# Starting product 2 of a tile inside the same tile: a new hand-written order of TensorE and ScalarE in a convolution and two-matmul kernel

## The chip, the cores and the metric

The kernel runs on one core of a Trainium2 chip. The metric is the time on the device, in microseconds (us), of one execution; smaller is better. A profile of one execution gives, for each engine, when every instruction started and ended. The engines are named as the profile names them: PE is TensorE (PEld its weight loads), ACT is ScalarE, DVE is VectorE, POOL is GpSimd, and SP is the engine whose queue issues the transfers (DMA).

## What is computed

The input `x` has 8 sequences of 4096 tokens with 192 features. Step one is a causal convolution over the last 7 tokens, with softmax-normalised weights of 8 heads (24 features each). Step two is a gated feed-forward layer on the 32768 tokens, with 2048 hidden features:

```python
w = exp(weight - max); w = w / (sum(w) + 1e-09)      # per head, 7 taps
x = einsum('hk,bskhg->bshg', w, x_unf)               # causal, zero-padded
h = x @ w_in                                         # 192 -> 2048
g = h * np.cos(h)
out = g @ w_out                                      # 2048 -> 192
```

## The kernel before

**Tiles and units.** The tokens are cut into 64 tiles of 512 (`T`, `NT`). Loads, the convolution and the transposition work on units of 1024 tokens, two tiles each (`U`, `TPU`), so there are 32 units.

**The way of one unit.** SP loads `x` (`load_unit`, `load_edges`). POOL casts it to bf16 (`cast_unit`, L174). PE convolves it as matmuls against a banded weight matrix (`conv_mm`, L185), in two parts of four heads; each part takes two PSUM banks and is cut in two steps, `c1` and `c2` (for a second part in the same tile `d1` and `d2`), between which the two row halves of PE change banks. ACT copies both banks out (`conv_out`, L200; written `ec` or `ed` in the order of ACT). POOL doubles the result (`double_unit`, L236), the DMA transposes it into `cT` (`turn_unit`, L242), and POOL mends the first six tokens of each 128 (`mend_edges`, L248).

**The way of one tile.** Product 1 makes eight slots `h0` to `h7` (`mm1`, L322), each of six matmuls of 512 columns and two PSUM banks. For each slot ACT computes the cosine (`s0` to `s7`, L328) and DVE multiplies it with h into the tile `g` (called g0 to g7 below, L332). Product 2 (`mm2_step`, L352) consists of 64 steps a tile, each of two matmuls of 192 columns that run side by side on the two row halves of PE. It runs in phases of 32 steps; in a phase the upper row half works on one half tile of the output and the lower row half on the half tile of the phase before. The results collect in two single-bank pools, `o_p` and `o_q`. ACT copies them out (`evac`, L364), `P` for half 0 and `Q` for half 1, and SP stores them.

**What sets the order.** Every engine works its own queue in order, and the order of the loop is written by hand: `PE_ORDER` and `ACT_ORDER` for tiles from 2 on, `PE_FIRST` and `ACT_FIRST` for tiles 0 and 1. In `PE_ORDER`, `m8` means eight steps of product 2.

```python
    PE_ORDER = "h0 c1 m8 c2 h1 m8 h2 h3 m16 | h4 h5 m8 h6 m12 h7 m12"
    ACT_ORDER = "P s0 ec s1 s2 s3 Q s4 s5 s6 s7"
```

In tile t the kernel before computes product 1 of tile t and product 2 of tile t-1 (upper rows) with the rest of tile t-2 (lower rows). Two more rounds follow the last tile.

**Buffers.** `h_pool` is a ring of three pairs of PSUM banks, taken in turn by the slots of product 1 and by the convolution. So a slot waits until the third one before it is free: `h2` waits for g0 of its own tile, because h0, the convolution and h1 hold the three pairs in between; `c1` waits for g6 of the tile before, and `h1` for g7. `cos_pool` and `gpool` have three buffers, the pools of `x`, its cast, `ct` and `cT` two each.

**Turns.** [...] Where they change banks, class `Turn` puts a small marker on SP's queue (L158): it waits for the last matmul of one half, and the first matmul of the other waits for it. The marker stands in SP's queue behind whatever transfers were issued before it.

Of the kernel before, what the change touches and what calls it, by code (L numbers as in the profile page):

```python
# [8 lines left out]
FP32 = mybir.dt.float32  # L9
# [7 lines left out]
def kernel(  # L17
# [8 lines left out]
    nc = tc.nc  # L26
# [5 lines left out]
    T = 512  # L32
    NT = NTOK // T
    NB = T // 128
    U = 1024
    NU = NTOK // U
    UB = U // 128
    UPS = S // U
    TPU = U // T
    NF = Dff // 128  # L40
    NP = NF // 2
# [25 lines left out]
    def load_edges(u):  # L67
        nc.sync.dma_start(out=x_tiles[u][:, UB, :],
                          in_=xf[u * U - 8 : u * U - 8 + U, :].rearrange("(n t) d -> n t d", t=128)[:, 0:16, :])
# [12 lines left out]
    HP = NP // 2  # L82
# [8 lines left out]
    def load_wo(q):  # L91
        for i in range(2):
            nc.sync.dma_start(out=wo_f[:, q * HP : (q + 1) * HP, i], in_=wo_src[:, q * HP : (q + 1) * HP, i])

    load_edges(1)
    load_wo(0)


    one = consts.tile([128, 128], FP32)
# [69 lines left out]
    def cast_unit(u, n0=0, n1=UB + 1):  # L169
        copy = nc.scalar.copy if u == 0 and n0 == 0 else nc.gpsimd.tensor_copy  # L170
        bf[u] = xb0 if u == 0 else xbf_pool.tile([128, UB + 1, D], BF16, name="x_bf")

        o = 1 if u == 0 else 0
        copy(out=bf[u][:, n0 + o : n1 + o, :].rearrange("p n (h k r) -> p (n h) k r", k=NC, r=R),  # L174
             in_=x_tiles[u][:, n0:n1, :].rearrange("p n (h r k) -> p (n h) k r", k=NC, r=R))
        if u and u % UPS == 0:
            nc.gpsimd.memset(bf[u][0:8, UB, :], 0.0)
        bf.pop(u - 2, None)
# [9 lines left out]
            rhs=bf[u][rows, n0:n1, h * G : (h + 1) * G].rearrange("p n (k r) -> p n k r", k=NC),  # L188
            skip_group_check=True, **flags)

    def conv_out(u, c, ps, n0, m0, m1, copy, double=False):

        for b in range(2):
            w0 = (2 * c + b) * 2 * R
            o = ct_tiles[u][:, m0:m1, :, :, w0 : w0 + 2 * R].rearrange("p n k t w -> p (n k) t w")
            i = ps[b][:, (m0 - n0) * 2 * G : (m1 - n0) * 2 * G].rearrange("p (m t w) -> p m t w", t=1, w=2 * R)
            if double:
                copy(o, i.to_broadcast([128, (m1 - m0) * NC, 2, 2 * R]))  # L198
            else:
                copy(o[:, :, 0, :], i[:, :, 0, :])  # L200

    def ring_banks():
        h = h_pool.tile([128, 2, T], FP32, name="h")
        return [h[:, 0, :], h[:, 1, :]]
# [4 lines left out]
    def conv_part(u, c, banks):  # L209


        ps = banks()
        sides = [slice(0, 64), slice(64, 128)]

        def mm(i, rows, **flags):
            return conv_mm(u, c, ps, i, sides[rows], 0, UB + 1, **{"start": False, "stop": False, **flags})

        mm(0, 0, start=True)
        mm(2, 1, start=True)
        turn = Turn()  # L220
        turn.mark(mm(1, 0), mm(3, 1))
        yield
        turn.wait(mm(2, 0), mm(0, 1))
        mm(3, 0, stop=True)
        mm(1, 1, stop=True)
        yield
        if c == 0 and u not in ct_tiles:
            ct_tiles[u] = ct_pool.tile([128, UB + 1, NC, 2, 64], BF16, name="ct")
        conv_out(u, c, ps, 0, 0, UB + 1, nc.scalar.copy)
        yield  # L230

    cT = {}

    def double_unit(u, n0=0, n1=UB + 1):
        ct = ct_tiles[u]
        nc.gpsimd.tensor_copy(out=ct[:, n0:n1, :, 1, :], in_=ct[:, n0:n1, :, 0, :])  # L236

    def turn_unit(u, n0=0, n1=UB + 1):
        ct = ct_tiles.pop(u)
        if u not in cT:  # L240
            cT[u] = cT_pool.tile([128, UB + 1, NC, 128], BF16, name="cT")
        nc.sync.dma_start_transpose(out=cT[u][:, n0:n1].rearrange("p n c k -> p (n c) k"),  # L242
                                    in_=ct[:, n0:n1].rearrange("p n c t k -> p (n c t k)"))
        cT.pop(u - 2, None)
# [52 lines left out]
    list(b)  # L297
    for half in range(2):
        list(across[half])
    double_unit(0, NB, UB)  # L300
    turn_unit(0, NB, UB)
    load_wo(1)
    nc.gpsimd.tensor_copy(out=w[:, :, HP:NP], in_=w_f[:, :, HP:NP])
    cast_unit(1)
    for q in range(2):
        nc.gpsimd.tensor_copy(out=wo[:, q * HP : (q + 1) * HP], in_=wo_f[:, q * HP : (q + 1) * HP])  # L306
    load_unit(2)
    load_edges(2)


    g_tiles = {}
# [23 lines left out]

    STEPS = 2 * NF

    def mm2_step(t, q):
        half, i = divmod(q, STEPS)
        f, si = divmod(i, 2)  # L340
        for r, (tt, b) in enumerate(((t - 1, half), (t - 1, 0) if half else (t - 2, 1))):
            if not 0 <= tt < NT:
                continue
            if r == 0 and i == 0:
                if tt < NT - 1:
                    o_ps[tt, b] = o_pools[b].tile([128, T], FP32, name="o_ps%d" % b)
                elif b == 0:

                    o_ps[tt, 0], o_ps[tt, 1] = ring_banks()
            rows = slice(64 * r, 64 * r + 64)  # L350
            s = 2 * b + si
            m = nc.tensor.matmul(out=o_ps[tt, b][:, si * D : (si + 1) * D],  # L352
                                 lhsT=g_tiles[tt][rows, f, s * 128 : (s + 1) * 128], rhs=wo[rows, f // 2, f % 2, :],
                                 start=(r == 0 and i == 0), stop=(r == 1 and i == STEPS - 1), skip_group_check=True)
            if r == 0 and i == STEPS - 1:
                turns[tt, b] = Turn()
                turns[tt, b].mark(m)
            if r == 1 and i == 0:
                turns.pop((tt, b)).wait(m)

    def evac(t, b):
        if b == 0:
            o_sb[t] = opool.tile([128, NB, D], FP32, name="o_sb")
        nc.scalar.copy(o_sb[t][:, 2 * b : 2 * b + 2, :].rearrange("p s d -> p (s d)"), o_ps.pop((t, b))[:, 0 : 2 * D])  # L364
# [6 lines left out]

    PE_ORDER = "h0 c1 m8 c2 h1 m8 h2 h3 m16 | h4 h5 m8 h6 m12 h7 m12"
    ACT_ORDER = "P s0 ec s1 s2 s3 Q s4 s5 s6 s7"

    PE_FIRST = ["h0 h1 h2 h3 h4 d1 h5 d2 h6 c1 h7 c2 |", "h0 m8 h1 m8 h2 h3 m16 | h4 c1 h5 m8 c2 h6 m12 h7 m12"]
    ACT_FIRST = ["s0 s1 s2 s3 s4 s5 ed s6 s7 ec", "s0 s1 s2 s3 s4 s5 ec s6 s7"]

    for t in range(NT + 2):  # L380
        u, second = divmod(t, TPU)
        cu, cc = (u + 2, 0) if second else (u + 1, 1)
        conv = {"c": conv_part(cu, cc, ring_banks if t else o_banks) if cu < NU else iter(())}
        if t == 0:
            conv["d"] = conv_part(1, 0, o_banks)
        act, done, h, step = (ACT_ORDER if t > 1 else ACT_FIRST[t]).split(), set(), {}, 0

        def flush():
            while act:
                k = act[0]  # L390
                need = {"P": "start", "Q": "|", "e": k[1:] + "2"}.get(k[0], "h" + k[1:])
                if need not in done:
                    return
                act.pop(0)
                if k == "P" and 0 <= t - 2 < NT:
                    evac(t - 2, 0)
                    if t == NT + 1:
                        store(t - 2, 0, 1)
                elif k == "Q" and 0 <= t - 2 < NT:
                    evac(t - 2, 1)  # L400
                elif k[0] == "e":
                    next(conv[k[1]], None)
                elif k[0] == "s" and t < NT:
                    gcu(t, int(k[1:]), h.pop(int(k[1:])))

        done.add("start")
        flush()
        for k in (PE_ORDER if t > 1 else PE_FIRST[t]).split():
            if k[0] == "h" and t < NT:
                h[int(k[1:])] = mm1(t, int(k[1:]))  # L410
            elif k[0] in conv:
                next(conv[k[0]], None)
            elif k[0] == "m":
                for q in range(step, step + int(k[1:])):
                    mm2_step(t, q)
                step += int(k[1:])
            done.add(k)
            flush()

            if k == ("|" if t == 0 else "h1") and second == 0 and cu < NU:  # L420
                double_unit(cu)
            if k == "|":
                if second == 0 and cu < NU:
                    turn_unit(cu)
                if 0 <= t - 2 < NT:
                    store(t - 2, 1 if t == NT + 1 else 0)
                if second == 1 and u + 3 < NU:
                    load_unit(u + 3)
                    load_edges(u + 3)
                if second == 0 and u + 2 < NU:  # L430
                    cast_unit(u + 2)
                if second == 0 and cu < NU:
                    mend_edges(cu)


# [28 lines left out]
```

## Time and profile before

The median of three runs is 734.67 us (734.67 to 735.29). The profiled execution spans 733.8 us.

| stage of the profile | us | PE busy | DVE busy | ACT busy |
|---|---|---|---|---|
| start to h0 of tile 2 (0 to 37.53) | 37.53 | 30.73 | 28.37 | 25.87 |
| tiles 2 to 62 (37.53 to 710.03) | 672.50 | 670.50 | 580.50 | 593.47 |
| tile 63 and the rest (710.03 to the end) | 23.77 | 19.24 | 10.92 | 11.06 |

Each line is one stretch of time with the microseconds that each engine was busy in it. Matmuls are pipelined and their ends are modelled by the profiler, so a busy PE can still hold waits. The starts of matmuls are therefore the better clock: two equal points of neighbouring tiles lie 11.04 us apart in the long middle stage.

### The profile page before, as it was taken

To read this page: it belongs to the slowest core of one execution; us is meant where nothing else is said; L and a number is where in the kernel's file an instruction comes from. 1 tells how busy PE (TensorE), PEld (TensorE's weight loads), DVE (VectorE), ACT (ScalarE), POOL (GpSimd) and SP (SyncE) were. 2 spreads that over 40 slices of the span, in tenths; PEclk is the share of its full clock that TensorE was granted. 3 is DMA by queue.
4 is the path that set the end of the run, shared out by engine and by line. 5 is a ranking of instruction groups with operands and counts; after the bars stand their busy time and mean duration, and the time that the engine had idled before them with its cause. 6 is when DMAs were issued, how large, how long until landed. Compare 5 with 4: busy or idle time off the path is not lost.

```text
span 733.8 us, 26364 instructions
## 1 busy us (share of the span) xinstructions
PE 720.5 (98%) x11835; PEld 546.5 (74%) x11835; DVE 619.8 (84%) x537; ACT 630.4 (86%) x781; POOL 150.0 (20%) x119
## 2 busy tenths in 40 slices
PE   7899999999999999999999999999999999999997
PEld 3577777777777777777777777777777777777776
DVE  6888888888888888888888888888888888888883
ACT  5888888888988988988988988988988988988883
POOL 4422220222210222211222211222211222211100
PEclk9999999999999999999999999999999999999999
DMA  9725435535335345446345345355345345343401
GB/s 226 202 74 142 112 101 142 108 105 142 108 106 142 101 113 141 88 127 142 97 116 142 97 117 141 93 121 127 107 123 142 89 125 141 88 126 94 93 24 67
DMA packets 184075, 86.04 MB, mean 117 GB/s; under 512 B 111642, under 2 KB 183194, under 8 KB 183962
## 3 DMA queue, kind: packets, MB, share of 16 engines
q1 hardware_dynamic: 183960, 84.36, 44.1%
q8 instruction: 92, 1.51, 0.8%
q14 instruction: 21, 0.17, 0.1%
q10 hardware_dynamic: 2, 0.00, 0.0%
HBM read 31.36 MB, written 25.17 MB: 77 GB/s over the span
## 4 chain that ended last, share of the span: by engine, by line
PE 97%; DVE 1%; ACT 1%; issue 1%
PE h L322 46%; PE o_ps L352 46%; PE h L185 3%; PE o_ps L107 1%; DVE g L332 1%; PE h L352 1%; ACT cs L328 0%; ACT ct L200 0%; ACT ct L198 0%; DVE cT L289 0%; ACT o_sb L364 0%; PE h L285 0%; PE o_ps L114 0%; PE o_ps L185 0%; DVE zero L102 0%
## 5 line engine op out<-in xcount | busy, mean ns | idle before, releaser
L332 DVE TENSOR_TENSOR g<-h,cs 128x1024 bf16<-128x1024 f32 x512 | 609.1, 1221 | 97.5 <-ACT cs L328 86.2
L328 ACT ACTIVATE cs<-h 128x1024 bf16<-128x1024 f32 x512 | 511.5, 1025 | 80.8 <-PE h L322 79.4
L352 PEld LDWEIGHTS <-g 64*128 64x128 bf16 x8192 | 362.4, 94 | 68.0 <-ACT ct L200 1.2
L322 PE MATMUL h<-cT,w 64*128 64x512 bf16 x3072 | 401.2, 376 | 5.5 <-DVE g L332 2.1
L352 PE MATMUL o_ps<-wo,g 64*128 64x192 bf16 x8064 | 403.2, 243 | 0.7 <-ACT ct L200 0.7
L322 PEld LDWEIGHTS <-w 64*128 64x128 bf16 x3072 | 166.5, 94 | 92.8 <-issue 15.4
L236 POOL COPY ct<-ct 128x1728 bf16<-128x1728 bf16 (+1 forms) x32 | 51.4, 1605 | 377.3 <-ACT ct L200 374.2
L174 POOL CAST x_bf<-x_f 128x1728 bf16<-128x1728 f32 (+1 forms) x32 | 80.7, 2521 | 0.1
L364 ACT COPY o_sb<-o_ps 128x384 f32<-128x384 f32 x126 | 60.4, 479 | 5.1 <-PE o_ps L352 2.4
L200 ACT CAST ct<-h 128x432 bf16<-128x432 f32 (+1 forms) x124 | 57.2, 513 | 2.2 <-PE h L185 0.6
L185 PE MATMUL h<-x_bf,band 64*128 64x216 bf16 (+1 forms) x512 | 45.5, 250 | 0.7 <-ACT ct L200 0.7
L248 POOL COPY cT<-cT 128x144 bf16<-128x144 bf16 x31 | 9.6, 309 | 153.7 <-DMA cT<-ct 69.3
L185 PEld LDWEIGHTS <-band 64*128 64x128 bf16 (+1 forms) x528 | 27.9, 94 | 15.1 <-issue 1.0
L107 PE MATMUL o_ps<-zero 128*128 128x512 bf16 x29 | 9.6, 502 | 1.3 <-DVE zero L102 1.3
L352 PE MATMUL h<-wo,g 64*128 64x192 bf16 x128 | 8.7, 243 | 0.6 <-ACT o_sb L364 0.6
L107 PEld LDWEIGHTS <-zero 128*128 128x128 bf16 x29 | 3.3, 121 | 6.3 <-issue 3.3
L364 ACT COPY o_sb<-h 128x384 f32<-128x384 f32 x2 | 1.0, 480 | 5.2 <-PE h L352 5.2
L306 POOL CAST wo<-wo_f 128x1536 bf16<-128x1536 f32 x2 | 2.9, 1469 | 3.3 <-DMA wo_f<-in_moe_w_out_dram 3.3
L255 DVE TENSOR_TENSOR prod<-mask,wn 128x2128 bf16<-128x2128 bf16 x1 | 2.4, 2376 | 0.1
L110 ACT ACT_TABLE_LOAD x1 | 1.3, 1283 | 1.3 <-PEq L448 1.3
L262 ACT COPY band<-prod 32x304 bf16<-32x304 bf16 x1 | 0.4, 444 | 2.2 <-DVE prod L258 2.2
L185 PE MATMUL o_ps<-x_bf,band 64*128 64x216 bf16 x16 | 1.7, 252 | 0.6 <-ACT ct L200 0.6
(41 smaller groups left out, 26.1 us busy)
## 6 DMA issues: line engine op xcount, KB each, us to landing
out_dram<-o_sb SPq DMA_DIRECT2D x63, 384.0 KB
x_f<-in_x_dram SPq DMA_DIRECT2D x31, 768.0 KB
x_f<-in_x_dram SPq DMA_DIRECT2D x31, 96.0 KB
w_f<-in_moe_w_in_dram SPq DMA_DIRECT2D x4, 384.0 KB
wo_f<-in_moe_w_out_dram SPq DMA_DIRECT2D x4, 384.0 KB
x_f<-in_x_dram SPq DMA_DIRECT2D x2, 384.0 KB
cT<-ct SPq DMA_TRANSPOSE x32
out_dram<-o_sb SPq DMA_DIRECT2D x2, 192.0 KB
```

The costliest lines, as they stand in the source:

```text
L107: nc.tensor.matmul(out=idle, lhsT=zero[:, 0:128], rhs=zero, start=True, stop=True)
L174: copy(out=bf[u][:, n0 + o : n1 + o, :].rearrange("p n (h k r) -> p (n h) k r", k=NC, r=R), in_=x_tiles[u][:, n0:n1, :].rearrange("p n (h ...
L185: return nc.tensor.matmul(out=ps[i // 2][:, 0 : (n1 - n0) * 2 * G].rearrange("p (n k i r) -> p i n k r", n=n1 - n0, k=NC, i=2)[:, i % 2], ...
L200: copy(o[:, :, 0, :], i[:, :, 0, :])
L236: nc.gpsimd.tensor_copy(out=ct[:, n0:n1, :, 1, :], in_=ct[:, n0:n1, :, 0, :])
L248: nc.gpsimd.tensor_copy(out=cT[u][:, 0:UB, :, 0 : K - 1], in_=cT[u][:, UB].rearrange("p c (n t) -> p n c t", t=16)[:, :, :, 8 : 8 + K - 1])
L306: nc.gpsimd.tensor_copy(out=wo[:, q * HP : (q + 1) * HP], in_=wo_f[:, q * HP : (q + 1) * HP])
L322: nc.tensor.matmul(out=h[:, i, :], lhsT=w[rows, k, j, :], rhs=c[rows, n0 : n0 + NB, k, :], start=(k == 0), stop=(k == NC - 1))
L328: nc.scalar.activation(out=cs, in_=h, func=AF.Sin, bias=math.pi / 2.0, scale=1.0)
L332: nc.vector.tensor_tensor(out=g_tiles[t][:, 2 * j : 2 * j + 2, :], in0=h, in1=cs, op=ALU.mult)
L352: m = nc.tensor.matmul(out=o_ps[tt, b][:, si * D : (si + 1) * D], lhsT=g_tiles[tt][rows, f, s * 128 : (s + 1) * 128], rhs=wo[rows, f // 2, ...
L364: nc.scalar.copy(o_sb[t][:, 2 * b : 2 * b + 2, :].rearrange("p s d -> p (s d)"), o_ps.pop((t, b))[:, 0 : 2 * D])
```

## The change

Product 2 is no longer counted by tile but by one running number of steps, so that its first eight steps for tile t (which need only g0 and g1) run after `h7` of the same tile. The rest of a tile's product 2 follows in the next tile, and one extra round less is needed at the end. PE and ACT get a new order. `p` marks the end of half 0 of a tile's output and `q` the end of half 1. The two banks of a convolution part are copied out by two separate entries (`ec1`, `ec2`), and the convolution of a unit is done a tile earlier: tiles 2u and 2u+1 convolve unit u+2, and its transposition is issued at `q` of tile 2u+2. In tile 0 both parts of unit 1 and 20 steps of product 2 are done, in tile 1 both parts of unit 2. The set-up changes accordingly: `load_wo(1)` is issued with the other first loads, the cast of unit 1 comes first in POOL's queue, and the transposition of the second half of unit 0 (`turn_unit(0, NB, UB)`) and the cast of `wo` move behind `d1` of tile 0.

```diff
-        conv_out(u, c, ps, 0, 0, UB + 1, nc.scalar.copy)
-        yield
+        for b in range(2):
+            conv_out(u, c, ps, 0, 0, UB + 1, nc.scalar.copy, banks=(b,))
+            yield
...
+    cast_unit(1)
     double_unit(0, NB, UB)
-    turn_unit(0, NB, UB)
-    load_wo(1)
-    nc.gpsimd.tensor_copy(out=w[:, :, HP:NP], in_=w_f[:, :, HP:NP])
-    cast_unit(1)
-    for q in range(2):
-        nc.gpsimd.tensor_copy(out=wo[:, q * HP : (q + 1) * HP], in_=wo_f[:, q * HP : (q + 1) * HP])
     load_unit(2)
     load_edges(2)
+    nc.gpsimd.tensor_copy(out=w[:, :, HP:NP], in_=w_f[:, :, HP:NP])
...
-        for r, (tt, b) in enumerate(((t - 1, half), (t - 1, 0) if half else (t - 2, 1))):
+        for r in range(2):
+            tt, b = divmod(phase - r, 2)
...
-    PE_ORDER = "h0 c1 m8 c2 h1 m8 h2 h3 m16 | h4 h5 m8 h6 m12 h7 m12"
-    ACT_ORDER = "P s0 ec s1 s2 s3 Q s4 s5 s6 s7"
-    PE_FIRST = ["h0 h1 h2 h3 h4 d1 h5 d2 h6 c1 h7 c2 |", "h0 m8 h1 m8 h2 h3 m16 | h4 c1 h5 m8 c2 h6 m12 h7 m12"]
-    ACT_FIRST = ["s0 s1 s2 s3 s4 s5 ed s6 s7 ec", "s0 s1 s2 s3 s4 s5 ec s6 s7"]
+    PE_ORDER = "h0 m7 c1 m6 c2 m4 h1 m7 q h2 h3 m12 h4 m10 h5 m10 h6 h7 p m8"
+    ACT_ORDER = "s0 ec1 ec2 s1 Q s2 s3 s4 s5 P s6 s7"
+    PE_FIRST = ["h0 h1 d1 h2 d2 h3 c1 h4 c2 h5 p m8 h6 m8 h7 m4",
+                "h0 m6 h1 m6 q h2 m8 h3 m4 d1 m4 d2 h4 m6 h5 c1 m6 c2 h6 h7 m4 p m8"]
+    ACT_FIRST = ["s0 s1 ed1 ed2 s2 s3 ec1 ec2 s4 s5 s6 s7", "s0 s1 s2 s3 ed1 ed2 s4 s5 ec1 ec2 P s6 s7"]
...
-        cu, cc = (u + 2, 0) if second else (u + 1, 1)
+        cu, cc = (u + TPU, second) if t >= TPU else (1 + t, 1)
...
+                if (t, k) == (0, "d1"):
+                    turn_unit(0, NB, UB)
+                    for q in range(2):
+                        nc.gpsimd.tensor_copy(out=wo[:, q * HP : (q + 1) * HP], in_=wo_f[:, q * HP : (q + 1) * HP])
...
+            if k == "q":
+                if second == 0 and t and u + 1 < NU:
+                    turn_unit(u + 1)
+                    mend_edges(u + 1)
+                if t == 1:
+                    turn_unit(1)
+                    mend_edges(1)
+                if second == 0 and u + 3 < NU:
+                    cast_unit(u + 3)
+                if second == 1 and t > 1 and cu < NU:
+                    double_unit(cu)
```

More of the change, by code (lines that the diff above doesn't have):

```diff
@@ L96 @@
     load_wo(0)
+    load_wo(1)
     one = consts.tile([128, 128], FP32)
@@ L189, in conv_mm, with conv_out @@
             skip_group_check=True, **flags)
-    def conv_out(u, c, ps, n0, m0, m1, copy, double=False):
-        for b in range(2):
+    def conv_out(u, c, ps, n0, m0, m1, copy, double=False, banks=(0, 1)):
+        for b in banks:
             w0 = (2 * c + b) * 2 * R
@@ L336, with mm2_step @@
     STEPS = 2 * NF
-    def mm2_step(t, q):
-        half, i = divmod(q, STEPS)
+    def mm2_step(q):
+        phase, i = divmod(q, STEPS)
         f, si = divmod(i, 2)
-        for r, (tt, b) in enumerate(((t - 1, half), (t - 1, 0) if half else (t - 2, 1))):
+        for r in range(2):
+            tt, b = divmod(phase - r, 2)
             if not 0 <= tt < NT:
@@ L344, in mm2_step @@
             if r == 0 and i == 0:
[L345 to L349, printed above, removed]
+                last = (tt, b) == (NT - 1, 1)
+                o_ps[tt, b] = ring_banks()[0] if last else o_pools[b].tile([128, T], FP32, name="o_ps%d" % b)
             rows = slice(64 * r, 64 * r + 64)
@@ L370 @@
     o_ps, o_sb, turns = {}, {}, {}
-    PE_ORDER = "h0 c1 m8 c2 h1 m8 h2 h3 m16 | h4 h5 m8 h6 m12 h7 m12"
-    ACT_ORDER = "P s0 ec s1 s2 s3 Q s4 s5 s6 s7"
-    PE_FIRST = ["h0 h1 h2 h3 h4 d1 h5 d2 h6 c1 h7 c2 |", "h0 m8 h1 m8 h2 h3 m16 | h4 c1 h5 m8 c2 h6 m12 h7 m12"]
-    ACT_FIRST = ["s0 s1 s2 s3 s4 s5 ed s6 s7 ec", "s0 s1 s2 s3 s4 s5 ec s6 s7"]
+    PE_ORDER = "h0 m7 c1 m6 c2 m4 h1 m7 q h2 h3 m12 h4 m10 h5 m10 h6 h7 p m8"
[3 more added lines that the diff above has]
+    ACT_FIRST = ["s0 s1 ed1 ed2 s2 s3 ec1 ec2 s4 s5 s6 s7", "s0 s1 s2 s3 ed1 ed2 s4 s5 ec1 ec2 P s6 s7"]
+    step = 0
     for t in range(NT + 2):
         u, second = divmod(t, TPU)
-        cu, cc = (u + 2, 0) if second else (u + 1, 1)
+        cu, cc = (u + TPU, second) if t >= TPU else (1 + t, 1)
         conv = {"c": conv_part(cu, cc, ring_banks if t else o_banks) if cu < NU else iter(())}
-        if t == 0:
-            conv["d"] = conv_part(1, 0, o_banks)
-        act, done, h, step = (ACT_ORDER if t > 1 else ACT_FIRST[t]).split(), set(), {}, 0
+        if t < TPU:
+            conv["d"] = conv_part(cu, 0, ring_banks if t else o_banks)
+        act, done, h = (ACT_ORDER if t > 1 else ACT_FIRST[t]).split(), set(), {}
         def flush():
@@ L390, in flush @@
                 k = act[0]
-                need = {"P": "start", "Q": "|", "e": k[1:] + "2"}.get(k[0], "h" + k[1:])
+                need = {"P": "p", "Q": "q", "e": k[1:2] + "2"}.get(k[0], "h" + k[1:])
                 if need not in done:
@@ L394, in flush @@
                 act.pop(0)
[L395 to L398, printed above, removed]
+                if k == "P" and 0 <= t - 1 < NT:
+                    evac(t - 1, 0)
                 elif k == "Q" and 0 <= t - 2 < NT:
@@ L404, in flush @@
                     gcu(t, int(k[1:]), h.pop(int(k[1:])))
-        done.add("start")
-        flush()
         for k in (PE_ORDER if t > 1 else PE_FIRST[t]).split():
@@ L412 @@
                 next(conv[k[0]], None)
+                if (t, k) == (0, "d1"):
+                    turn_unit(0, NB, UB)
+                    for q in range(2):
+                        nc.gpsimd.tensor_copy(out=wo[:, q * HP : (q + 1) * HP], in_=wo_f[:, q * HP : (q + 1) * HP])
             elif k[0] == "m":
                 for q in range(step, step + int(k[1:])):
-                    mm2_step(t, q)
+                    mm2_step(q)
                 step += int(k[1:])
+            elif k[0] == "p":
+                assert step % (2 * STEPS) == 0
+            elif k[0] == "q":
+                assert step % (2 * STEPS) == STEPS
             done.add(k)
             flush()
[L420 to L433, printed above, removed]
+            if k == "q":
[9 more added lines that the diff above has]
+                    double_unit(cu)
+                if t == NT + 1:
+                    store(NT - 1, 1, 2)
+            if k == "p":
+                if t < NT + 1 and 0 <= t - 2:
+                    store(t - 2)
+                if t == NT:
+                    store(NT - 1, 0, 1)
+                if second == 1 and u + 4 < NU:
+                    load_unit(u + 4)
+                    load_edges(u + 4)
+        if t == 0:
+            double_unit(1)
+            load_unit(3)
+            load_edges(3)
+            cast_unit(2)
+        if t == 1:
+            double_unit(2)
+            cast_unit(3)
 _INS = ['x', 'weight', 'moe_w_in', 'moe_w_out']
```

## The prediction

> **What bounds the kernel now.** I read the page's busy times and chain first. PE carries the end; DVE and ACT follow at 84% and 86%.
>
> ```profile
> span 733.8 us, 26364 instructions
> ...
> PE 720.5 (98%) x11835; PEld 546.5 (74%) x11835; DVE 619.8 (84%) x537; ACT 630.4 (86%) x781; POOL 150.0 (20%) x119
> ...
> PE 97%; DVE 1%; ACT 1%; issue 1%
> ```
>
> Is PE full, or waiting inside its busy time? The chain in a window of the middle tells; its columns are start, length, what.
>
> ```profile
> 195.26 0.03 issue
> 195.29 1.47 PE h L322 x12
> 196.76 1.32 PE o_ps L352 x32
> 198.08 1.29 PE h L322 x12
> ...
> 203.31 0.65 PE h L322 x6
> 203.96 0.18 PE h L185 x4
> ...
> 206.33 1.47 PE h L322 x12
> ```
>
> The same twelve matmuls cost 1.47 (h2, h3) and 1.29 (h4, h5): 0.18 more, after 0.03 of issue, once in every tile of 206.33 - 195.29 = 11.04 us. The timeline of that window says why.
>
> ```profile
> 203.13 0.83 PE L322 MATMUL h<-cT,w 64*128 64x512 bf16 x6
> 204.00 1.02 ACT L328 ACTIVATE cs<-h 128x1024 bf16<-128x1024 f32 x1 [0.15 <-PE h L322]
> 205.05 1.22 DVE L332 TENSOR_TENSOR g<-h,cs 128x1024 bf16<-128x1024 f32 x1 [0.41 <-ACT cs L328]
> 206.33 1.47 PE L322 MATMUL h<-cT,w 64*128 64x512 bf16 x12
> ```
>
> h0 starts at 203.13, its cosine 0.86 later, g0 1.06 after that, and h2 starts 0.05 after g0's end. So h2 waits for the bank pair of h0: the loop slot, cosine, product, next slot takes 0.86 + 1.06 + 1.28 (206.33 - 205.05) = 3.20 us, and PE has less work than that to put between. The page lists this wait under "issue", 0.20 each time. Last come the two ends of the run, from two windows of the timeline.
>
> ```profile
> 15.66 2.12 PE L322 MATMUL h<-cT,w 64*128 64x512 bf16 x18 [1.14 <-DVE cT L289]
> 16.86 2.52 POOL L174 CAST x_bf<-x_f 128x1728 bf16<-128x1728 f32 x1
> 28.49 3.47 SPq L242 DMA_TRANSPOSE cT<-ct  x1
> 37.53 0.83 PE L322 MATMUL h<-cT,w 64*128 64x512 bf16 x6
> ...
> 710.03 0.83 PE L322 MATMUL h<-cT,w 64*128 64x512 bf16 x6
> 729.90 0.48 ACT L364 COPY o_sb<-h 128x384 f32<-128x384 f32 x1 [2.88 <-PE h L352]
> ```
>
> Product 1 starts at 15.66; h0 of tile 2 at 37.53; h0 of tile 63 at 710.03; the last copy at 729.90.
>
> [...] pairs start 0.216 and 0.0825 us apart. [...] here the two of a pair start 0.02 apart. [...]
>
> **The change, part by part.**
>
> *Work.* PE keeps all its matmuls. Per tile: 8 slots x 0.6475 (1.29/2) = 5.18; 64 steps x 0.0825 = 5.28; convolution 2 x 0.185 = 0.37; sum 10.83. Before, 10.83 + 0.21 = 11.04.
>
> *New order, tiles 2 to 59.* Counting from h0: h0 0; m7 0.65; c1 1.23; m6 1.41; c2 1.91; m4 2.09; h1 2.42; m7 3.07; h2 3.65; h3 4.29; m12 4.94; h4 5.93; h5 7.41; h6 8.88; h7 9.53; m8 10.17; end 10.83. Cosines start 0.86 after a slot, or when ACT is free (0.92 from cosine to cosine, 0.42 from cast to what follows, about 0.4 after P or Q, an estimate from its 0.48): s0 0.86, ec 2.35 and 2.77, s1 3.28, Q 4.25, s2 4.65, s3 5.57, s4 6.80, s5 8.27, P 9.2, s6 9.74, s7 10.66. Products start 1.06 later, at least 1.137 apart (4.82 for four starts and one end): g1 4.34, g2 5.71, g3 6.84, g4 7.98, g5 9.32, g6 10.80, g7 11.93, next g0 13.07, thus 2.24 in its own tile. A bank pair is free 1.28 after its g starts:
>
> - h2 needs g0: 2.24 + 1.28 = 3.52, wanted 3.65. The old wait is gone.
> - h4 to h7 need g1 to g4: 5.62, 6.99, 8.12, 9.26; wanted 5.93, 7.41, 8.88, 9.53. Next h0 needs g5: 10.60 of 10.83.
> - next c1 needs g6: 12.08, wanted 10.83 + 1.23 = 12.06. A wait of 0.02. Next h1 needs g7: 13.21 of 13.25.
>
> So the period is 10.85, and the tightest loop moves to h6, s6, g6, c1. The other waits are covered: P is done 9.7, m8 takes its bank at 10.17; Q is done 4.75, m12 needs it at 4.94. The early m8 reads only g0 and g1, finished by 5.6. SP's markers: at c1 the marker takes 0.21 after c1 (before: c1 ended 203.97, marker 204.17), and m6 gives 0.495; at phase ends two slots (1.3) stand between. The transposition holds SP 3.4 us from 3.9 to 7.3, before the next marker at 8.9; stores and loads go from 9.1 to 11.3, before c1's at 12.2. Separate copies, convolution and doubling a tile earlier add no work and are off PE's path.
>
> 58 x 10.85 = 629.3. Tiles 60 to 62 have no convolution: 10.46 each, 31.4. Together 660.7 instead of 672.5: **-11.8**.
>
> *Tile 0 and 1.* Here the change costs. POOL now casts unit 1 first, and that load lands at 16.16 in the trace's DMA records. Cast 16.25 to 18.77 (2.52), doubling to 19.6, second half of `w` to 21.0, `wo` to 22.4 and 23.8. h0, h1 at 15.66, 16.31; d1 waits for the cast, 18.82; h2 19.0, d2 19.65, h3 19.84. ACT queues ed1 and ed2 (20.10, 20.51) ahead of s2 (20.93), which without them could start at 19.9. c1 needs the copies, 21.05; SP's marker for c1 stands behind the transposition (19.6 to 21.9), c2 22.0; s3 21.85, ec 22.8 and 23.2, s4 23.6, s5 24.5; h5 23.27 (g2), m8 23.92, h6 24.58, m8, h7 25.94 (g4), m4 26.58. Tile 0 ends at 26.91 with g7 at 28.08.
> Tile 1: h0 27.08, h1 28.39 (g6), h2 29.69 (g7), m8, h3 31.0, d1 31.98. The transposition of unit 1 holds SP from 29.95 to 33.4 and d2's marker with it: d2 33.5 in place of 32.5. Then h4 33.69, s4 34.77, h5 34.83, h6 37.1 (g4), h7 38.25, m4 to 39.23. P comes before s6 on ACT but waits for this m4: P 39.46, m8 needs its bank, 39.99, so h0 of tile 2 at 40.65; s6 39.87 instead of 37.96, g6 ends 42.15, c1 at 42.2 = 40.98 + 1.23. Tile 2 acts as if begun at 41.0: 41.0 - 37.53 = **+3.5**. SP's issue of 6144 descriptors ahead of d1's marker I take as done by 18 (about 2000 were outstanding at 12.96 before; 4132 done at 17.84); were it 20, h0 of tile 2 comes about 1 later.
>
> *End.* Tile 63: 10.46; 20 steps later the last quarter needs g7, 12.85 + 0.33 = 13.18; marker 0.25 and 32 steps 2.64: 16.07; marker and 32 lone steps (before 2.80): 19.05; copy 0.25 + 0.48; and 3.4 from the last copy's end to the end of the span, as now: 23.2 against 23.77: **-0.6**.
>
> Sum: -11.8 + 3.5 - 0.6 = -8.9; 734.67 - 8.9 = 725.8, say 726.
>
> **Rivals.**
>
> - *The wait moves and stays.* The h6 to c1 loop has 3.18 of PE work against 3.20: no slack. If P delays s6, or a wait costs 0.2 more, the period is 11.04 again, the start still costs 3.5: about 734.67 + 3.5 - 0.6 = 737.6, slower. For: c1 and h1 have 0.02 and 0.04. Against: P is ready at 9.11, and from s5 at 8.27 to s6 at 9.74 there are 1.47 for a cosine and a copy. A half-size loss, 0.08 a tile, gives 58 x 0.08 = 4.6: 730.5.
> - *The start is free.* ACT and DVE catch up in tiles 0 and 1 and tile 2 begins at 38: 722.8. For: 1.65 of product 2 moves into tile 0, where PE idles. Against: DVE sets the pace there, and s2, d2 and s6 each wait.
> - *DVE becomes the bound.* Its floor is 8 x 1.137 = 9.1 a tile, ACT's about 9; neither reaches 10.83. A time near 734.7 would need some loss that cancels -8.9 by chance.
>
> **How the numbers follow.** Forecast 726: 0.60. Free start, 723: 0.18. Half-size loss, 730.5: 0.12. Wait moved, 737.6: 0.07. No change: 0.03. Range 720.5 to 732.5: the first three, with 2 on either side for ACT's gaps and SP's queue. Faster 0.90, same 0.03, slower 0.07.
>
> **What would show it.** Right: h2 starts without a gap, the period is 10.83 to 10.87, a short gap stands at c1; h0 of tile 2 near 40.6, with P ahead of s6 waiting at about 39.4 and d2 behind SP's transposition. Wrong: a period of 10.95 or more, with "DVE g" as releaser at c1 or h1; or tile 2 before 39 or after 43.

## The result and the profile after

The changed kernel takes 728.79 us (median of four runs, 727.85 to 729.58) against 734.81 for the kernel before, measured beside it on the same chip. The ratio is 0.9916, with a 95% interval of 0.9899 to 0.9934. The change makes the kernel faster by 6.0 us, inside the forecast range and 2.8 us short of the forecast.

The first lines of the page after, then the start of its fourth part (the chain of work that ended last, by engine):

```profile
span 727.0 us, 26343 instructions
...
PE 711.9 (98%) x11835; PEld 531.6 (73%) x11835; DVE 614.3 (84%) x537; ACT 617.2 (85%) x781; POOL 149.8 (21%) x119
...
PE 94%; SPq 2%; DMA 2%; DVE 1%; ACT 1%; POOL 1%; issue 0%; DVEq 0%; ACTq 0%; POOLq 0%
```

PE has the same 11835 matmuls and carries the end as before. The share "issue" (1% before) is gone, and SPq and DMA have come in with 2% each: the middle has lost its wait, and the start has gained some.

The middle of the run, from the chain in a window (start, length, what):

```profile
206.32 0.65 PE h L320 x6
206.97 0.58 PE o_ps L349 x14
207.55 0.20 PE h L186 x4
207.75 0.49 PE o_ps L349 x12
208.25 0.18 PE h L186 x4
208.43 0.33 PE o_ps L349 x8
208.76 0.65 PE h L320 x6
209.41 0.58 PE o_ps L349 x14
209.99 1.29 PE h L320 x12
...
215.22 1.29 PE h L320 x12
216.51 0.66 PE o_ps L349 x16
217.17 0.65 PE h L320 x6
```

h2 and h3 at 209.99 now take 1.29, as h6 and h7 at 215.22 do; they took 1.47 before. No issue line is left. The first step of the convolution takes 0.20 where the second takes 0.18: this is the wait of 0.02 at `c1`, which begins at 207.39 in the timeline, 0.05 after DVE's g6 ends at 207.34. The period is 217.17 - 206.32 = 10.85 us.

The start, from the timeline of the changed kernel (start, busy time, engine, line, operation; in brackets the idle time before it and what ended it):

```profile
14.60 1.47 PE L320 MATMUL h<-cT,w 64*128 64x512 bf16 x12 [1.14 <-DVE cT L291]
16.76 2.50 POOL L175 CAST x_bf<-x_f 128x1728 bf16<-128x1728 f32 x1 [5.14 <-DMA x_f<-in_x_dram]
...
19.32 0.36 PE L186 MATMUL o_ps<-x_bf,band 64*128 64x216 bf16 x4 [3.24 <-POOL x_bf L175]
...
19.50 1.43 PE L320 MATMUL h<-cT,w 64*128 64x512 bf16 x6
20.07 3.82 SPq L244 DMA_TRANSPOSE cT<-ct  x1
24.01 0.36 PE L186 MATMUL o_ps<-x_bf,band 64*128 64x216 bf16 x4 [0.34 <-SPq L159]
...
31.64 4.24 SPq L244 DMA_TRANSPOSE cT<-ct  x1
35.99 0.36 PE L186 MATMUL h<-x_bf,band 64*128 64x216 bf16 x4 [1.70 <-SPq L159]
...
41.95 0.48 ACT L361 COPY o_sb<-o_ps 128x384 f32<-128x384 f32 x1 [1.90 <-PE o_ps L349]
42.33 2.86 ACT L326 ACTIVATE cs<-h 128x1024 bf16<-128x1024 f32 x3
42.48 0.83 PE L349 MATMUL o_ps<-wo,g 64*128 64x192 bf16 x16 [0.58 <-ACT o_sb L361]
43.14 0.83 PE L320 MATMUL h<-cT,w 64*128 64x512 bf16 x6
```

PE waits 3.24 us for POOL's cast in front of `d1` (19.32). Then the six matmuls of h2 take 1.43 us where six others take 0.83. SP issues a transposition for 3.82 us, and `c2` of tile 0 starts at 24.01, just after it; the next holds `d2` of tile 1 until 35.99 in the same way. `P` waits 1.90 for PE, s6 stands behind it (42.33), and h0 of tile 2 starts at 43.14.

Why h2 is slow is in the windows view (stretch, length, busy time of PE, PEld, DVE, ACT and POOL, then the granted clock of PE, the DMA share and GB/s). The first three lines are of the changed kernel, the last is the whole start of the kernel before:

```profile
14.00:19.50 5.50, 1.65 (x16) 0.87 (x18) 2.81 (x3) 1.94 (x2) 2.74 (x2) 1.00 1.10 333
19.60:23.00 3.40, 3.40 (x24) 1.86 (x21) 0.00 (x0) 1.67 (x3) 3.40 (x4) 0.50 1.40 309
23.00:26.00 3.00, 2.53 (x27) 1.45 (x25) 2.35 (x2) 2.70 (x5) 1.87 (x2) 1.00 0.88 136
...
0.00:37.53 37.53, 30.73 (x292) 17.76 (x293) 28.37 (x40) 25.87 (x39) 17.36 (x23) 1.00 0.88 210
```

For 3.4 us after its pause of 3.24 us PE runs at half clock, 0.50 from 19.6 to 23.0. The kernel before shows 1.00 over its whole start; it put h2 to h4 before its first convolution step.

The end, from the timeline (h0 of tile 63 and the last copy):

```profile
704.00 0.83 PE L320 MATMUL h<-cT,w 64*128 64x512 bf16 x6
...
723.11 0.48 ACT L361 COPY o_sb<-h 128x384 f32<-128x384 f32 x1 [2.35 <-PE h L349]
```

To compare the stages, let E be the moment at which tile 2 acts as if begun: h0 of tile 3 (54.28 here) less one period. It is 43.43, later than h0 of tile 2 at 43.14 because the `c1` of tile 2 waited.

| stage, us | before | predicted | after |
|---|---|---|---|
| start, up to E | 37.53 | 41.0 | 43.43 |
| tiles 2 to 62 | 672.5 | 660.7 | 660.6 |
| tile 63 and the rest | 23.77 | 23.2 | 23.0 |

The sum of the differences is +5.9 - 11.9 - 0.8 = -6.8, the difference of the two spans (733.8 and 727.0). The profiled run of before took 735.56, 0.75 above the median of 734.81, so between medians it is 6.0. E is read from one profile of each kernel; the last experiment shows how far it varies.

### The profile page after: what moved, and what is told of

It is laid out like the page before. It is cut to its first block, busy times and chain, and to the rows that moved or that the text cites. A ratio compares the mean times of both kernels' runs of the same rounds, so it can differ in the third digit from the quotient of the medians.

```text
span 727.0 us, 26343 instructions
## 1 busy us (share of the span) xinstructions
PE 711.9 (98%) x11835; PEld 531.6 (73%) x11835; DVE 614.3 (84%) x537; ACT 617.2 (85%) x781; POOL 149.8 (21%) x119
## 4 chain that ended last, share of the span: by engine, by line
PE 94%; SPq 2%; DMA 2%; DVE 1%; ACT 1%; POOL 1%; issue 0%; DVEq 0%; ACTq 0%; POOLq 0%
PE o_ps L349 46%; PE h L320 44%; PE h L186 3%; DMA wo_f<-in_moe_w_out_dram 2%; DVE g L330 1%; SPq L244 1%; ACT cs L326 1%; PE h L349 0%; SPq L85 0%; SPq L74 0%; POOL wo L412 0%; POOL w L306 0%; SPq L68 0%; DVEq L478 0%; ACT ct L201 0%
## 5 line engine op out<-in xcount | busy, mean ns | idle before, releaser
L349 PE MATMUL o_ps<-wo,g 64*128 64x192 bf16 x8128 | 424.8, 243 | 1.1 <-ACT o_sb L361 0.6
L320 PEld LDWEIGHTS <-w 64*128 64x128 bf16 x3072 | 154.7, 94 | 87.6 <-issue 4.1
L186 PEld LDWEIGHTS <-band 64*128 64x128 bf16 (+1 forms) x528 | 23.4, 95 | 10.9 <-issue 4.5
L349 PE MATMUL h<-wo,g 64*128 64x192 bf16 x64 | 5.8, 243 | 0.0
L201 ACT CAST ct<-o_ps 128x432 bf16<-128x432 f32 x4 | 1.9, 522 | 4.2 <-PE o_ps L186 4.2
```

Source lines behind the costliest of these rows:

```text
L186: return nc.tensor.matmul(out=ps[i // 2][:, 0 : (n1 - n0) * 2 * G].rearrange("p (n k i r) -> p i n k r", n=n1 - n0, k=NC, i=2)[:, i % 2], ...
L320: nc.tensor.matmul(out=h[:, i, :], lhsT=w[rows, k, j, :], rhs=c[rows, n0 : n0 + NB, k, :], start=(k == 0), stop=(k == NC - 1))
```

## The experiments

Each run has its profile, so E can be read in each. In all profiles of kernels that keep the middle of the changed kernel, the span less E is 683.5 to 683.6 us: what an edit of the start does to the profiled span is what it does to E.

**h2 early again.** The theory: the new order gains because 24 steps and the convolution stand between h0 and h2 instead of 16 and the convolution. The rival: it gains because product 2 overlaps its own tile.

```diff
-    PE_ORDER = "h0 m7 c1 m6 c2 m4 h1 m7 q h2 h3 m12 h4 m10 h5 m10 h6 h7 p m8"
+    PE_ORDER = "h0 m5 c1 m4 c2 m1 h1 m6 q h2 h3 m12 h4 m10 h5 m10 h6 h7 p m16"
```

The last `m8` of tile 1 becomes `m16` too.

> Everything of the change stays (product 2 begins in the same tile, conv a tile ahead, bank-by-bank copies), but 16 steps instead of 24 stand between h0 and h2, as before the change; the eight go to the tile's last slot (m16). Theory (the gain is the wait at h2): h2 is wanted at 2.99 us after h0, its banks come free at 3.20, so the wait of 0.2 us is back, the period is 11.04 again and the time rises by 58 x 0.19 = 11 us over the changed kernel, to about 740. Rival (the gain comes from the overlap of a tile's two products as such): no more than 1 us of difference, 728 to 730.

Measured: 740.3 us (739.83 to 740.71), ratio to before 1.0072 [1.0055, 1.0089]. The chain in the same window of this run:

```profile
198.81 0.65 PE h L320 x6
...
201.30 0.50 PE o_ps L349 x12
201.80 0.03 issue
201.83 1.47 PE h L320 x12
...
209.85 0.65 PE h L320 x6
```

The 1.47 and the issue line are back. The chain counts h0 from 198.81, 0.18 after its start in the timeline (198.63). From there to h2 there are 201.83 - 198.63 = 3.20 us, the loop of the prediction to the hundredth, and the period is 11.04 again. Product 2 overlaps its own tile even more here, by 16 steps, and gains nothing by it: the kernel is 5.1 us slower than before, about the cost of the start. The rival falls.

**The kernel before with a new order only.** Can the middle's gain be had without product 2 in its own tile?

```diff
-    PE_ORDER = "h0 c1 m8 c2 h1 m8 h2 h3 m16 | h4 h5 m8 h6 m12 h7 m12"
-    ACT_ORDER = "P s0 ec s1 s2 s3 Q s4 s5 s6 s7"
+    PE_ORDER = "h0 c1 m8 c2 m4 h1 m8 h2 m12 | h3 h4 m8 h5 m8 h6 m8 h7 m8"
+    ACT_ORDER = "P s0 ec s1 s2 Q s3 s4 s5 s6 s7"
```

> The kernel before with another order in tiles from 2 on and nothing else: PE h0 c1 m8 c2 m4 h1 m8 h2 m12, then h3 h4 m8 h5 m8 h6 m8 h7 m8, and Q before s3 on ACT. Product 2 does not begin in its own tile. Between h0 and h2 stand 20 steps instead of 16, so h2 is wanted at 3.32 us and g0's banks are free at 3.20; the tightest loop is h6 to c1, which lacks 0.08. Theory (only the distance between h0 and h2 counts): period about 10.91, 59 x 0.13 = 7.7 us less than before, with the start of before: about 727. Rival (the wait goes only if product 2 begins in the same tile): no faster than 734.

Measured: 732.53 us, 0.9968 [0.9957, 0.9979]; the period is 10.99 (in its chain one h0 starts at 202.26 and the next at 213.25). Its timeline at the start of a tile:

```profile
213.07 0.83 PE L322 MATMUL h<-cT,w 64*128 64x512 bf16 x6
...
213.55 0.47 ACT L364 COPY o_sb<-o_ps 128x384 f32<-128x384 f32 x1
213.79 0.36 PE L185 MATMUL h<-x_bf,band 64*128 64x216 bf16 x4
...
214.08 0.84 PE L352 MATMUL o_ps<-wo,g 64*128 64x192 bf16 x16
214.73 0.36 PE L185 MATMUL h<-x_bf,band 64*128 64x216 bf16 x4
```

h2 no longer waits, but two smaller waits have taken its place. h0 starts at 213.07 and `c1` at 213.79, 0.72 later where a slot needs 0.65: 0.07 lost, where `c1` needs the bank pair of g6 (DVE ends it at 213.74). The next product 2 starts 0.29 after `c1` where 0.185 is enough, 0.06 after the copy `P` (213.55 + 0.47): about 0.1 lost on its bank. 10.83 + 0.07 + 0.1 gives the 10.99 to 0.01. Both expectations miss: the loop to `c1` was foreseen, at 0.08, the one of `P` was not. This order alone brings a third of a per cent. Starting eight steps in the tile before leaves more steps to stand between h0 and `c1` and moves `P` away from h0, so that all loops fit at once in the changed kernel. Only this one other order was tried: that none reaches 10.85 without product 2 in its own tile is not shown.

**Zero matmuls in the pause.** They add nothing to the result; they keep PE busy while it waits for POOL's cast.

```diff
-    PE_FIRST = ["h0 h1 d1 h2 d2 h3 c1 h4 c2 h5 p m8 h6 m8 h7 m4",
+    PE_FIRST = ["h0 h1 w d1 h2 d2 h3 c1 h4 c2 h5 p m8 h6 m8 h7 m4",
...
+            elif k == "w":
+                rest = o_pools[0].tile([128, T], FP32, name="o_ps0")
+                for _ in range(15):
+                    nc.tensor.matmul(out=rest, lhsT=zero[:, 0:128], rhs=zero, start=True, stop=True)
```

> 15 extra matmuls of zeros between h1 and d1 of tile 0 fill TensorE's 3.2 us of waiting for the cast of unit 1. Clock theory (the start is 2.4 us later than forecast because TensorE drops to half clock from 19.6 to 23.0 us after that pause): the half-clock record is gone, and tile 2 begins 1 to 2 us earlier than 43.4, 727 to 728 us in all. Rival (c2 of tile 0 stands behind SP's transposition anyway, which issues until 23.9): matmuls run at full clock, but c2 still starts near 24.0 and tile 2 near 43.4; no difference in time.

Measured: 729.21 us (727.2 to 730.44), 0.9917 [0.9895, 0.994]. The windows view of this run, the same stretch as above, then three lines of its timeline:

```profile
19.60:23.00 3.40, 2.94 (x32) 1.41 (x29) 0.56 (x1) 2.46 (x4) 3.40 (x3) 1.00 1.16 298
...
19.84 2.36 SPq L244 DMA_TRANSPOSE cT<-ct  x1
...
22.32 0.39 PE L186 MATMUL o_ps<-x_bf,band 64*128 64x216 bf16 x4
...
30.45 3.87 SPq L244 DMA_TRANSPOSE cT<-ct  x1
```

The clock stays at 1.00, 32 matmuls run in the stretch in place of 24, and E is 41.88 instead of 43.43. These 1.55 us can't be put down to the half clock alone. Both transpositions held SP for less time in this run as well (2.36 and 3.87 us for 3.82 and 4.24), though the edit doesn't touch them, and `c2` starts at 22.32, just after the first. In the changed kernel PE was ready for `c2` 0.34 us before SP let it start at 24.01: full clock alone would have left it near 24.0, a short transposition alone near 23.7 (an estimate from these lines). The two lay side by side, and neither's share is isolated. The profiled run took 727.2, three others 728.3 to 730.4, so a gain of time is not shown. Only the mean clock is kept of those: 0.999, 0.997 and 0.996 for 728.29, 730.44 and 730.13. Where they lost clock stays open.

**Markers ahead of the transpositions.** The transposition of unit 0 is issued after `c1`'s marker, and that of unit 1 at the end of tile 0, ahead of `d1` and `d2` of tile 1.

```diff
-                if (t, k) == (0, "d1"):
+                if (t, k) == (0, "c1"):
                     turn_unit(0, NB, UB)
+                if (t, k) == (0, "d1"):
...
-                if t == 1:
-                    turn_unit(1)
-                    mend_edges(1)
...
             load_edges(3)
+            turn_unit(1)
             cast_unit(2)
+            mend_edges(1)
```

> The transposition of unit 0 is issued after the marker of c1 of tile 0 instead of before it, that of unit 1 at the end of tile 0 instead of at q of tile 1, so that neither c2 of tile 0 nor d2 of tile 1 waits behind it on SP. Marker theory (the start lost its time there): c2 of tile 0 starts near 23 instead of 24.0, d2 of tile 1 loses its wait of 1.7 us, tile 2 begins near 41 instead of 43.4, time 726 to 727. Rival (DVE's chain of eight products sets the start, or the half clock): less than 0.5 us gained.

Measured: 726.34 us (726.13 to 726.72), 0.9882 [0.9867, 0.9896]. All four runs lie below every run of the changed kernel. Its timeline:

```profile
22.70 1.52 SPq L244 DMA_TRANSPOSE cT<-ct  x1
...
22.95 0.42 PE L186 MATMUL o_ps<-x_bf,band 64*128 64x216 bf16 x4
...
26.54 3.96 SPq L244 DMA_TRANSPOSE cT<-ct  x1
...
33.53 0.41 PE L186 MATMUL h<-x_bf,band 64*128 64x216 bf16 x4
```

`c2` of tile 0 starts at 22.95, during the transposition and not after it. `d2` of tile 1 starts at 33.53, 2.46 earlier than in the changed kernel, though the cast of unit 1 let `d1` begin 0.65 later here (19.97). E is 41.18. This profile has no stretch at half clock either, so the 2.25 of E is not all the markers'. The gain of time, 1.5 us against the last experiment and 2.5 against the result, is not the half clock's absence alone, though: the three other runs have a mean clock of 0.996, 0.998 and 0.996, where runs of the changed kernel have 0.994 to 0.999, and they took 726.1 to 726.7 like the profiled one at 1.000.

**`P` earlier in tile 1.** The last four steps of half 0 move ahead of h6 and h7.

```diff
-                "... d2 h4 m6 h5 c1 m6 c2 h6 h7 m4 p m8"]
+                "... d2 h4 m6 h5 c1 m6 c2 m4 p h6 h7 m8"]
```

> In tile 1 the last four steps of the phase and p stand before h6 instead of after h7, so that ACT's copy P no longer holds s6 and s7, and the last eight steps find their bank free. Theory: s6 starts right after h6 (near 40.5 instead of 42.3), the 0.6 us wait of TensorE for P is gone, tile 2 begins near 42.0 instead of 43.4, time about 727.4. Rival (DVE or the next copies hold tile 2 anyway): no difference.

Measured: 729.44 us (727.72 to 730.42), 0.9921 [0.9903, 0.9939]: no gain, as the rival had it. At one mean clock, 0.999, a run of it took 727.72 and one of the changed kernel in the last experiment 727.73. The timeline around `P`:

```profile
39.22 0.53 ACT L361 COPY o_sb<-o_ps 128x384 f32<-128x384 f32 x1
...
39.48 1.63 POOL L238 COPY ct<-ct 128x1728 bf16<-128x1728 bf16 x1 [1.11 <-ACT ct L201]
39.78 2.15 ACT L326 ACTIVATE cs<-h 128x1024 bf16<-128x1024 f32 x2
...
41.05 2.54 POOL L175 CAST x_bf<-x_f 128x1728 bf16<-128x1728 f32 x1
...
43.65 0.36 PE L186 MATMUL h<-x_bf,band 64*128 64x216 bf16 x4 [0.89 <-POOL x_bf L175]
```

`P` starts with no wait, s6 follows at 39.78 (42.33 before the edit), and h0 of tile 2 is 1.8 earlier, at 41.35; 0.7 of that was there at `d2` of tile 1 already (35.30 for 35.99), in a profile whose clock read 1.00 from 16.5 to 24.5. But `c1` of tile 2 then waits for POOL, which casts unit 3 (41.05) behind the doubling of unit 2 (39.48). E is 42.40, 1.0 less than in the changed kernel's profile. One wait gave way to the next.

**Three edits together.** The markers, `P` early, and on POOL the cast of unit 3 ahead of that doubling.

```diff
         if t == 1:
-            double_unit(2)
             cast_unit(3)
+            double_unit(2)
```

> Three edits of the first two tiles together: the transpositions behind the markers (as in e3), p of tile 1 before h6 (as in e4), and on POOL the cast of unit 3 ahead of the doubling of unit 2. In e4 the copy P no longer held s6, but c1 of tile 2 started at 43.65, 0.05 us after POOL's cast of unit 3 had ended (43.60), which stands behind the doubling. Theory (that cast was the new wait of e4): P early now pays its 1 us, tile 2 begins near 40.0 instead of 41.2 in e3, time about 725.2. Rival (DVE's products hold tile 2): no better than e3, 726.3.

Measured: 724.84 us (724.31 to 726.2), 0.9868 [0.9855, 0.9882]; E is 38.97. With POOL's cast out of the way `P` early pays: 2.2 us of E less than with the markers alone, of which 0.76 stands at `d2` of tile 1 already (32.77 for 33.53), and 1.5 us of time, or 1.0 when each run is set against the kernel before beside it. The cast moved by itself was not run.

**Start rearranged.** The same three edits; h2 and h3 go before `d1` again, product 2 of tile 0 starts after h7, and the second half of `w` is cast ahead of unit 1.

```diff
-    PE_FIRST = ["h0 h1 d1 h2 d2 h3 c1 h4 c2 h5 p m8 h6 m8 h7 m4",
+    PE_FIRST = ["h0 h1 h2 h3 d1 h4 d2 h5 c1 h6 c2 h7 p m8 m8 m4",
...
-    ACT_FIRST = ["s0 s1 ed1 ed2 s2 s3 ec1 ec2 s4 s5 s6 s7", ...
+    ACT_FIRST = ["s0 s1 s2 s3 ed1 ed2 s4 s5 ec1 ec2 s6 s7", ...
```

> e5 and a tile 0 nearer to that of before: the second half of w is cast first on POOL, the cast of unit 1 after it, h2 and h3 come before d1, s2 and s3 before ed1, and product 2 starts after h7. Theory (in tile 0 the cosines and products stand still while TensorE waits for the cast of unit 1): DVE's products follow each other without the pause after g1, g7 of tile 0 starts near 27.2 instead of 29.2, tile 2 begins near 39 and the time is about 724. Rival (the loads and POOL set the start of tile 1): as e5.

Measured: 723.82 us (723.38 to 724.82), 0.9854 [0.984, 0.9867]; E is 38.04. By the median this is the best version, 1.0 us below the three edits, with ranges that overlap; which of its moves brings that was not separated. It is faster than both kernels. It keeps the middle's gain whole, and its E is only 0.5 above the 37.53 of before.

**The changed kernel once more.**

> The changed kernel once more beside these. 728 to 730; whether its half-clock record after the pause of tile 0 comes in this execution too.

Measured: 727.81 us, 0.9912 [0.9899, 0.9926]; four runs of 727.62, 727.73, 727.88 and 729.87. The longest is the profiled one, and its windows view shows why:

```profile
19.00:22.50 3.50, 3.50 (x26) 1.98 (x27) 0.00 (x0) 1.43 (x3) 3.50 (x4) 0.51 1.23 324
22.60:36.00 13.40, 10.51 (x128) 7.05 (x124) 11.69 (x10) 9.97 (x12) 5.41 (x3) 1.00 0.70 135
36.20:39.50 3.30, 3.30 (x28) 1.89 (x26) 1.18 (x1) 1.96 (x3) 0.31 (x1) 0.50 0.36 80
```

Two stretches at half clock, the second after the wait at `d2` of tile 1 (2.12 us here); E is 44.53. Span and time differ by 1.8 us, so the runs of 727.62 to 729.87 put E anywhere from about 42.3 to 44.5 (an estimate that takes the rest as in the profiles). A single profile of this kernel overstates or understates its start by about a microsecond, and differences of E that small between single profiles prove nothing.

## Why the prediction was right, and where it was off

The direction and the mechanism were right; the step that was off is the term of the start, +3.5, which measured +5.9 in the first profile and +7.0 in the second. Tile 2 came at 43.14, just past the 43 that the prediction had named as a sign of being wrong; the range of the time was wide enough for that.

- *The wait of h2 and the new period.* Right. 10.85 was forecast and measured, with the 0.02 at `c1`; the three tiles without convolution took 10.45 to 10.47 (forecast 10.46). The first experiment shows that the gain hangs on the distance from h0 to h2: undo it and the old period is back. The second shows that this distance alone is not enough. The tightest loop did not take more than its 0.02, so the rivals "the wait moves and stays" and its half-size form fall, and DVE and ACT did not become the bound (84% and 85%).
- *The order of PE and ACT at the start.* Right in kind. `d2` of tile 1 stood behind SP's transposition, and s6 behind `P` behind PE's last four steps, as forecast. The markers' experiment takes the first away. Taking away the second alone gained nothing, because POOL's cast stood ready as the next wait; the prediction did not see that one. SP's issue ahead of `d1`, which the prediction took as done by 18, ended at 18.9 and cost nothing: `d1` waited for the cast until 19.32.
- *The size of the start.* Off by 2.4. Product 1 began at 14.60, a microsecond earlier than reckoned, and all of that was lost and more. Three terms were too small. The cast of unit 1 was put at 16.25, after the landing at 16.16, and it started at 16.76: the landing read from before was that of the large load, and the cast also waited for the edges, whose last record is at 16.71. From h2 to `d2` 0.65 was reckoned, at full clock, and it took 1.19 (19.50 to 20.69) at half clock; the prediction read the granted clock nowhere, though its own order left PE idle from h1 to `d1`. The transpositions were put at 2.3 and 3.4 us of SP, as the kernel before shows them, and took 3.82 and 4.24. So `c2` of tile 0 came at 24.01 instead of 22.0, `d2` of tile 1 at 35.99 instead of 33.5, `P` at 41.95 instead of 39.46, h0 of tile 2 at 43.14 instead of 40.65. From `c2` on, the delay is the same to half a microsecond.
- *How it divides.* That stays open. At `c2` of tile 0 the half clock and SP's longer hold lay side by side, and the run with zero matmuls, 1.55 of E less, was without both. The markers' run was 2.25 of E less, with no half clock either; of it the gain of time, 1.5 to 2.5 us, is shown. Why the same transposition holds SP for 3.82 us in the changed kernel and 2.36 in the run with zero matmuls is not known.
- *The end.* -0.6 was forecast, -0.8 came. Both kernels still run two rounds after the last tile; what is shorter is the product 2 left for them, 88 steps for 96.
- *The rival "the start is free".* Wrong for the kernel as changed, yet within reach of it: with three edits E is 38.97, with the rearranged start 38.04, and the time 723.8 is close to that rival's 722.8.

## What to carry to other kernels

Where a ring of buffers makes one slot wait, count the microseconds of other work between the slot and the one whose buffer it takes, for every loop of the ring at once: a new order pays when all of them fit, and two loops short by 0.07 and 0.1 us took back 0.16 of the 0.21 us a tile in the kernel before with a new order. A prologue written anew for a better steady state has to be priced as its own kernel, with the queue of every engine walked through in its order (here `d2` of tile 1 waited 1.70 us for SP's marker behind a transposition, and `c1` of tile 2 0.89 us for POOL's cast behind a doubling). When one wait is taken out and the time stands still, look for the next in line before giving the edit up: `P` early paid only once POOL's cast was out of the way.

## What the runs showed of the hardware

In three of the profiles a pause of PE was followed by a stretch at half clock. In the changed kernel PE stood idle for 3.24 us, and the granted clock was 0.50 for 3.4 us, from 19.6 to 23.0. In the run with h2 early a pause of 2.98 us was followed by it too (0.50 from 20.5 to 23.5), and in the second profile of the changed kernel one of 3.12 us (0.50 from 19.5 to 21.5) and one of 2.12 us (0.50 from 36.2 to 39.5). It does not always follow: after 2.85 us in the markers' run, 2.36 with `P` early and 2.42 with the three edits, the clock read 1.00 up to 24.5. So the length of the pause alone does not decide it, since 2.12 us brought the half clock and 2.85 did not. What decides it was not shown.

Product 1 started between 14.36 us (the second profile of the changed kernel) and 15.66 (the kernel before), 14.60 in the first profile of the changed kernel.

The time for which a transposition holds SP's queue varies too. That of the second half of unit 0, issued at `d1` of tile 0, took 3.82 us in the changed kernel and 2.36 in the run with zero matmuls; in the three runs that issue it after `c1` it took 1.52 or 1.53. That of unit 1 took from 3.87 (zero matmuls) to 4.76 us (three edits).
